# Full-width products near four-column-tile products issued as four 32-column tiles

## The chip, the cores and the metric

The kernel runs on one core of a Trainium2 chip. The metric is the device time of one execution in microseconds (us). Before the change it is 253.65 us (median of three runs, 252.73 to 253.94). Most executions of one kernel agree within about 1%; a run that is over 1.5% above the fastest of its kernel is called slow and is left out of ratios.

## The reference

Two branches of a sequence of 2048 tokens with 640 channels are mixed by a gate:

```python
g = sigmoid((x * gate_w).sum(-1, keepdims=True))
a = _A_ref(...)     # 32 heads of 20 channels, 4 segments of 512 tokens:
                    # softmax(q k^T + mask) v inside a segment, plus a memory of the
                    # earlier segments, then  o @ wo   (the output projection)
b = _B_ref(...)     # irfft2(rfft2(x) * (w_r + 1j * w_i))   (the spectral filter)
return g * a + (1 - g) * b
```

## The kernel before

The program is recorded as operations with priorities, a list scheduler puts them in an order for each engine, and they are then emitted with semaphores. One TensorE operation is a list of matmuls:

```python
def mms(self, items, r, w, prio, name="", extra=0.0):
    cost = sum(max(c * PECOL, 27.0) for _, c in items) + extra
    def f(e):
        h = None
        for th, _ in items:
            o_, l_, r_, st, sp_, kw = th()
            h = e.matmul(o_, l_, r_, start=st, stop=sp_, **kw)
        return h
    return self.Sc.op({"pe": (f, cost, 110.0)}, r=r, w=w, prio=prio, name=name)
```

Every matmul reaches the chip as two instructions, a weight load and a matmul (the trace before has 3248 weight loads and, as a few records are missing, 3226 of the 3248 matmuls). TensorE is used in three tilings: full (128 rows by 128 columns), four row tiles (the scores `qk`, contraction over 20 channels), and four column tiles. In column tiles four matmuls with 32 weight columns each run side by side: in the trace before they start a median 3 ns apart, and a set of four, 320 columns wide, starts 136 ns after the one before it, as a full matmul of 320 columns does. The end of the filter uses them, because each 32-row strip needs another moving operand:

```python
# finish_tile: one 128-row output tile, in two halves of 320 columns
for q in range(4):                                   # "Fb": four column tiles
    # out strip 32q..32q+31  <-  fb[:, 32*(4a+q) : +32]^T  @  G[4a+q][:, half]
    ... {"tile_position": (0, 32 * q), "skip_group_check": True}
for c in range(5):                                   # "oproj", same PSUM bank
    if s < 3:   # one full matmul, 320 wide
        ... oT.ap(c * P, [1, P]), self.wo.ap(c * D + hf * 320, [1, 320])
    else:       # last segment: four column tiles
        ... {"tile_position": (0, 32 * q)}
```

The probability-times-value products (`pv`) are full matmuls that are only 21 wide: 40 of them for a group of four heads.

```python
# pv_group, one item: weights = a 128x128 block of probabilities, moving = 21 columns of values
(self.ps(bank, i*88 + hh*VW, [1, DH+1]), self.ex.ap(... , [1, P]), va.ap(... , [1, DH+1]), ...)
```

The softmax here doesn't subtract the row's maximum and nothing guards it: scores larger than these inputs give would overflow.

## Time and profile before

| | before |
|---|---|
| time, median of 3 | 253.65 us |
| matmuls in the program | 3248 |
| changes of tiling between neighbouring matmuls | 216 |
| last stretch, 197.4 to 249.3 us | TensorE without a break |

PE is TensorE's matmul side and PEld its weight loads. In the page, the chain of waits is followed back from the last instruction; its first line gives shares of the span by engine:

```profile
PE 57%; DVE 19%; DMA 10%; ACT 5%; SPq 3%; issue 3%; POOL 1%; ACTq 0%; DVEq 0%
```

The listing of the same chain in order of time (start, length, what) has its longest piece near the end:

```profile
197.38 51.87 PE psum L593 x867
```

867 matmuls follow each other with nothing else on the chain, so TensorE time saved after 197 us shortens the kernel. The windows view of the kernel before (length, then busy us and instruction count per engine, granted clock, DMA share, GB/s) agrees:

```profile
core 0: us, PE busy (x) PEld busy (x) DVE busy (x) ACT busy (x) POOL busy (x), PEclk, DMA share, GB/s
197.00:240.00 43.00, 42.77 (x642) 24.75 (x640) 24.94 (x66) 34.58 (x30) 18.15 (x28) 1.00 0.35 76
...
230.00:240.00 10.00, 10.00 (x199) 6.50 (x199) 5.43 (x14) 7.57 (x6) 5.85 (x9) 1.00 0.29 84
```

What a change of tiling costs is read from the timeline of TensorE before (start, length, instruction, weights and columns in use, shape, count):

```profile
216.80 0.32 PE L593 MATMUL psum<-G,fbg 128*32 128x320 bf16 x4
217.05 0.85 PE L593 MATMUL psum<-wo,oT 128*128 128x320 bf16 x5
217.84 0.32 PE L593 MATMUL psum<-G,fbg 128*32 128x320 bf16 x4
218.09 0.31 PE L593 MATMUL psum<-wo,oT 128*128 128x320 bf16 x1
```

In this trace a full matmul of 512 columns takes 216 ns from its start to the next one's, and one of 320 columns takes 136 ns (80 ns for 192 columns, which is the 2.4 GHz of the prediction). Four column tiles of 320 columns, where more column tiles follow, take 136 ns too, but the full matmul behind them here starts 0.25 us after them. The missing 0.11 us is the change of tiling. Behind five full matmuls it is the same (0.79 us for 5 x 0.136).

The page's line for an instruction queue (packets, MB, share of 16 engines) is taken for TensorE's: its 25 packets of 16 KB are one for about 260 of the 2 x 3248 weight loads and matmuls:

```profile
q8 instruction: 25, 0.41, 0.7%
```

### The profile page before, as it was taken

The page shows a single profiled execution, that of the slowest core. Times are in us where ns is not written, and L with a number is a line of the kernel's source. Part 1 is how long each engine was busy: PE and PEld are TensorE (multiplying, and loading weights), DVE is VectorE, ACT ScalarE, POOL GpSimd, SP SyncE. Part 2 cuts the span into 40 slices and gives each one's busy share as a digit, 9 for nine tenths or more (in the row PEclk, how much of TensorE's full clock was granted, in tenths as well). Part 3 has the DMA queues.
Part 4 walks back from the last instruction along what each step waited for, and adds up shares of the span by engine and source line. Part 5 has one row for each costly group of instructions (what it writes and reads, how often), then busy time and mean ns, then how long its engine had stood idle before and what let it go on. Part 6 is the DMA issues. An engine that isn't in the chain of part 4 may idle for free.

```text
span 253.9 us, 7958 instructions
## 1 busy us (share of the span) xinstructions
PE 235.9 (93%) x3226; PEld 138.4 (55%) x3248; DVE 202.2 (80%) x556; ACT 203.1 (80%) x208; POOL 114.4 (45%) x175
## 2 busy tenths in 40 slices
PE   7999999989999989989989999999997999999993
PEld 2344556544665547644646566545563656456583
DVE  0789799759998899999999988979999984625543
ACT  2397499958999898999988889889889798788710
POOL 8004735523533336745255747535575532416400
PEclk9999999979999999999999999999999999999998
DMA  7997979599479366656238385313666303464223
GB/s 173 358 355 216 216 173 225 121 205 221 101 112 227 79 168 189 159 125 191 64 96 182 70 204 141 101 44 114 134 169 153 70 3 84 92 115 94 78 68 103
DMA packets 56003, 36.76 MB, mean 145 GB/s; under 512 B 31792, under 2 KB 52256, under 8 KB 55968
## 3 DMA queue, kind: packets, MB, share of 16 engines
q1 hardware_dynamic: 54272, 35.45, 57.6%
q10 hardware_dynamic: 1696, 0.82, 1.2%
q8 instruction: 25, 0.41, 0.7%
q14 instruction: 10, 0.08, 0.2%
HBM read 19.86 MB, written 9.84 MB: 117 GB/s over the span
## 4 chain that ended last, share of the span: by engine, by line
PE 57%; DVE 19%; DMA 10%; ACT 5%; SPq 3%; issue 3%; POOL 1%; ACTq 0%; DVEq 0%
PE psum L593 57%; ACT ex L1183 4%; DMA xsb<-in_A_x_dram 4%; DVE Pt L1333 3%; DMA pkn<-phk 3%; SPq L622 2%; DVE va L1089 2%; DVE xsb L913 1%; SPq L620 1%; DMA tt<-tab_tt 1%; DVE Cp L603 1%; DVE qu L603 1%; DVE xf L908 1%; DMA q_scr<-qu 1%; DMA Wt<-in_B_w_i_dram 1%
## 5 line engine op out<-in xcount | busy, mean ns | idle before, releaser
L1183 ACT ACTIVATE ex<-psum 128x2048 bf16<-128x2048 f32 x80 | 150.3, 1879 | 17.9 <-PE psum L593 17.3
L1186 POOL TENSOR_SCALAR_AFFINE_SELECT ex<-ex 128x512 bf16<-128x512 bf16 x128 | 80.7, 647 | 110.7 <-ACT ex L1183 109.3
L593 PEld LDWEIGHTS psum<-va,ex 128*128 128x128 bf16 x1280 | 36.6, 96 | 7.2 <-POOL ex L1186 2.5
L593 PE MATMUL psum<-va,ex 128*128 128x21 bf16 x1280 | 38.6, 173 | 1.7 <-POOL ex L1186 0.6
L593 PE MATMUL psum<-qp,kp 20*128 20x512 bf16 (+3 forms) x512 | 31.9, 303 | 1.5 <-ACT ex L1183 0.6
L593 PE MATMUL psum<-wv,xT 128*128 128x141 bf16 (+1 forms) x160 | 28.0, 306 | 1.5 <-DVE qu L603 0.6
L1333 DVE TENSOR_TENSOR Pt<-psum,Wt 128x642 bf16<-128x642 f32 x32 | 25.6, 822 | 2.7 <-PE psum L593 1.6
L593 PE MATMUL psum<-xT,wk 128*128 128x512 bf16 (+1 forms) x127 | 25.6, 384 | 2.1 <-DVE qu L603 0.8
L593 PE MATMUL psum<-xT,wq 128*128 128x512 bf16 (+1 forms) x132 | 26.5, 380 | 0.7 <-issue 0.4
L593 PE MATMUL psum<-wo,oT 128*128 128x320 bf16 x120 | 22.1, 301 | 0.0
L593 PEld LDWEIGHTS psum<-qp,kp 20*128 20x128 bf16 x512 | 9.0, 92 | 20.4 <-ACT ex L1183 10.7
L593 PEld LDWEIGHTS psum<-wv,xT 128*128 128x128 bf16 x160 | 13.0, 98 | 10.5 <-issue 1.2
L593 PE MATMUL psum<-big,Cp 128*128 128x321 bf16 (+1 forms) x96 | 17.2, 302 | 1.0 <-DVE eo L603 0.4
L1054 ACT ACTIVATE et<-qu 128x512 bf16<-128x512 bf16 x25 | 15.7, 635 | 2.5 <-DVE qu L603 2.4
L603 DVE CAST ot<-psum 128x320 bf16<-128x320 f32 x19 | 9.1, 490 | 10.6 <-PE psum L593 9.4
L1089 DVE TENSOR_TENSOR va<-psum,ebx 128x500 bf16<-128x500 f32 (+1 forms) x32 | 15.2, 482 | 2.8 <-PE psum L593 1.7
L593 PEld LDWEIGHTS psum<-xT,wk 128*128 128x128 bf16 (+1 forms) x140 | 9.7, 98 | 13.5 <-issue 2.7
L1379 DVE TENSOR_TENSOR G<-eo,psum 128x320 bf16<-128x320 f32 x32 | 14.7, 476 | 2.5 <-PE psum L593 2.4
L593 PEld LDWEIGHTS psum<-xT,wq 128*128 128x128 bf16 (+1 forms) x140 | 10.0, 97 | 11.3 <-issue 1.3
L1218 DVE TENSOR_TENSOR on<-psum,rs 128x320 bf16<-128x320 f32 x32 | 15.5, 483 | 0.3
L593 PE MATMUL psum<-big,Ac 128*128 128x161 bf16 (+2 forms) x96 | 14.5, 257 | 1.3 <-DVE qu L603 0.9
L593 PE MATMUL psum<-tt,Yt 128*128 128x256 bf16 (+1 forms) x96 | 15.0, 273 | 0.3
(80 smaller groups left out, 357.2 us busy)
## 6 DMA issues: line engine op xcount, KB each, us to landing
tt<-tab_tt SPq DMA_DIRECT2D x16, 256.0 KB, 2.9
xsb<-in_A_x_dram SPq DMA_DIRECT2D x8, 320.0 KB, 6.9
qp<-q_scr SPq DMA_DIRECT2D x28, 80.0 KB
kp<-k_scr SPq DMA_DIRECT2D x28, 80.0 KB
o_scr<-on SPq DMA_DIRECT2D x12, 160.0 KB
out_dram<-ot SPq DMA_DIRECT2D x12, 160.0 KB
q_scr<-qu SPq DMA_DIRECT2D x6, 256.0 KB
k_scr<-qu SPq DMA_DIRECT2D x6, 256.0 KB, 2.8
```

Source lines behind the costliest of these rows:

```text
L593: h = e.matmul(o_, l_, r_, start=st, stop=sp_, **kw)
L603: alts["dve"] = (lambda e: e.tensor_copy(dst(), src()), 75 + 1.04 * n, 85.0)
L620: return e.dma_start_transpose(d_, s_)
L622: return e.dma_start(d_, s_)
L908: self.either(lambda e, r=r, op=op: e.tensor_tensor(xf.ap(r * 642, [321, 2], [1, 320]), xs.ap(o, [D, 2], [1, 320]), xs.ap(o + 320, [D, 2], ...
L1054: self.one("act", lambda e: e.activation(et.ap(0, [1, L]), qsl(), ACT.Exp), L, [qb], [b("et", pi_)], late, name="phi_exp")
L1089: self.one("dve", lambda e: e.tensor_tensor(va.ap(i * H * VW + h0 * VW, [VW, nh], [1, DH]), self.ps(bank, 0, [DH, nh], [1, DH]), self.ebx. ...
L1183: self.one("act", lambda e: e.activation(dst(), src(), ACT.Exp, scale=SC), 4 * width, [bank], [self.exb(s, g, j) for g, j in outs], prio - ...
L1186: self.one("pool", lambda e, g=g, j=j: e.affine_select(self.ex.ap(self.exo(s, g) + JOFF[j], [1280, 4], [1, P]), self.ex.ap(self.exo(s, g) ...
L1218: self.one("dve", lambda e, rs=rs, bank=bank, g=g: e.tensor_tensor(on.ap(80 * g, [D, 4], [DH, 4], [1, DH]), self.ps(bank, 0, [88, 4], [VW, ...
L1333: self.one("dve", lambda e, ri=ri, Pt=Pt, Wt=Wt, bank=bank: e.tensor_tensor(Pt.ap(ri * 322, [644, 2], [1, KD]), self.ps(bank, 0, [0, 2], [ ...
L1379: self.one("dve", lambda e, q=q, n2=n2, bank=bank, eo=eo: e.tensor_tensor(self.G.ap(n2 * D + 639 * q, [1 - 2 * q, 320]), eo.ap(q, [1, 320] ...
```

## The change

The intent is to change tiling less often. After scheduling, a greedy pass gives each group of operations that share PSUM banks a mode, full (0) or column tiles (2), with one unit of cost for each change of tiling and 0.03 for each operation in column tiles. A full matmul in mode 2 is issued as four of 32 weight columns. Some modes are fixed: warm-up and gate are full, scores are row tiles, filter product, last projection and a few query and key products are column tiles. The output projection of the first three segments shares its PSUM bank with the filter product and so becomes column tiles with it; the greedy pass chooses for the groups without a fixed member.

```diff
+    def set_modes(self):
...
+        def cost(ops):
+            ids = {o.id for o in ops}
+            c = 0.03 * sum(o.mode == 2 for o in ops)
+            for o in ops:
+                p, n = nbr[o.id]
+                c += (p is not None and p.mode != o.mode) + (n is not None and n.id not in ids and n.mode != o.mode)
+            return c
...          (greedy: runs of 1 to 3 groups are set to 0 or 2 while the cost falls)
     def mms(...):
                 o_, l_, r_, st, sp_, kw = th()
-                h = e.matmul(o_, l_, r_, start=st, stop=sp_, **kw)
+                if mode >= 0 or op.mode != 2:
+                    h = e.matmul(o_, l_, r_, start=st, stop=sp_, **kw)
+                    continue
+                pitch, m = l_.ap[1]
+                for q in range(0, m, 32):
+                    n = min(32, m - q)
+                    dst = bass.AP(tensor=o_.tensor, offset=o_.offset + q * o_.ap[0][0], ap=[[o_.ap[0][0], n]] + [list(d) for d in o_.ap[1:]])
+                    wt = bass.AP(tensor=l_.tensor, offset=l_.offset + q * pitch, ap=[list(l_.ap[0]), [pitch, n]])
+                    h = e.matmul(dst, wt, r_, start=st, stop=sp_, **{**kw, "tile_position": (0, q), "skip_group_check": True})
...
                 self.Sc.schedule({"qk": [0, 1, 2, 3], "gen": [4, 5, 6, 7]}, self.PLAN)
+                self.Sc.set_modes()
```

More of the change, by code (lines that the diff above doesn't have):

```diff
@@ L48 @@
     __slots__ = ("id", "alts", "preds", "succs", "prio", "banks", "nbytes", "npred", "eng", "t0", "t1",
-                 "stamp", "need_inc", "dyn", "first", "outside", "name", "dma", "key", "xfer", "lock")
+                 "stamp", "need_inc", "dyn", "first", "outside", "name", "dma", "key", "xfer", "lock", "mode")
 class Sched:
@@ L68, in op @@
         o.alts, o.prio, o.nbytes, o.name, o.dma = alts, prio, nbytes, name, dma
-        o.xfer, o.lock = xfer, lock
+        o.xfer, o.lock, o.mode = xfer, lock, 0
         o.key = self.keys.setdefault((self.group, name), len(self.keys))
@@ L325, in schedule @@
         self.nsem = nsem
+    def set_modes(self):
+        pe = [o for o in self.order if o.eng == "pe"]
+        banks = {}
+        for o in pe:
+            for b in o.banks:
+                banks.setdefault(id(b), []).append(o)
+        flex = [g for g in banks.values() if all(o.mode < 0 for o in g)]
+        for g in banks.values():
+            for o in g:
+                if o.mode < 0:
+                    o.mode = 2 if any(q.mode == 2 for q in g) else 0
+        nbr = {o.id: (p, n) for p, o, n in zip([None] + pe[:-1], pe, pe[1:] + [None])}
+        def cost(ops):
[5 more added lines that the diff above has]
+            return c
+        moved = True
+        while moved:
+            moved = False
+            for i, g in enumerate(flex):
+                for k in (1, 2, 3):
+                    ops = [o for q in flex[i:i + k] for o in q]
+                    old = [o.mode for o in ops]
+                    c0 = cost(ops)
+                    for m in (0, 2):
+                        for o in ops:
+                            o.mode = m
+                        c1 = cost(ops)
+                        if c1 < c0 - 1e-9:
+                            c0, old, moved = c1, [m] * len(ops), True
+                    for o, m in zip(ops, old):
+                        o.mode = m
     def pe_slow(self, now, occ):
@@ L582, in ps, with mms @@
                        ap=[[4096, np_]] + [list(q) for q in dims])
-    def mms(self, items, r, w, prio, name="", extra=0.0):
+    def mms(self, items, r, w, prio, name="", extra=0.0, mode=-1):
         cost = sum(max(c * PECOL, 27.0) for _, c in items) + extra
@@ L592, in f @@
                 o_, l_, r_, st, sp_, kw = th()
-                h = e.matmul(o_, l_, r_, start=st, stop=sp_, **kw)
-            return h
-        return self.Sc.op({"pe": (f, cost, 110.0)}, r=r, w=w, prio=prio, name=name)
+                if mode >= 0 or op.mode != 2:
[7 more added lines that the diff above has]
+                    h = e.matmul(dst, wt, r_, start=st, stop=sp_, **{**kw, "tile_position": (0, q), "skip_group_check": True})
+            return h
+        op = self.Sc.op({"pe": (f, cost, 110.0)}, r=r, w=w, prio=prio, name=name)
+        op.mode = mode
+        return op
     def copy_alts(self, dst, src, n, engines=("act", "dve"), scale=None):
@@ L816, in warm_up @@
             self.mms([(lambda k=k: (self.ps(bank, 0, [1, L]), t.ap(0, [1, P]), t.ap(P, [1, L]), True, True, {}), 1000)],
-                     [b("warm"), bank], [], -1.0, name="warm")
+                     [b("warm"), bank], [], -1.0, name="warm", mode=0)
     NWARM = 16
@@ L973, in proj_direct @@
                 items.append((th, L / 4))
-            self.mms(items, [b("w" + which + "a"), xb[c], bank], [], prio + (0.0 if c < 3 else 0.45), name="projd")
+            self.mms(items, [b("w" + which + "a"), xb[c], bank], [], prio + (0.0 if c < 3 else 0.45), name="projd", mode=2)
         self.Sc.op(self.copy_alts(lambda: pad.ap(g * L, [1, L]), lambda: self.ps(bank, 0, [1, L]), L),
@@ L1001, in gate @@
             items.append(((lambda n_=n_, part=part: (self.ps(bank, 0, [1, P], np_=4), part(), self.fcat.ap(P, [1, P]), n_ == 0, n_ == 1, {})), P))
-        self.mms(items, [b("hi", s), b("lo", s), b("fcat"), bank], [], prio + 4.0, name="gateT")
+        self.mms(items, [b("hi", s), b("lo", s), b("fcat"), bank], [], prio + 4.0, name="gateT", mode=0)
         self.one("dve", lambda e: e.tensor_copy(self.gT.ap(0, [1, P], np_=4), self.ps(bank, 0, [1, P], np_=4)), P, [bank], [b("gT")],
@@ L1171, in qk_unit @@
                 outs.append((g, j))
-        o = self.mms(items, rb + [bank], [], prio - self.QK_LEAD, name="qk")
+        o = self.mms(items, rb + [bank], [], prio - self.QK_LEAD, name="qk", mode=1)
         fn, occ, lat = o.alts["pe"]
@@ L1427, in finish_tile @@
                 items.append((th, 80))
-            self.mms(items, [b("fbg", s % 3), bank] + last + [b("G", 4 * a + q, hf) for q in range(4)], [], prio, name="Fb", extra=80.0)
+            self.mms(items, [b("fbg", s % 3), bank] + last + [b("G", 4 * a + q, hf) for q in range(4)], [], prio, name="Fb", extra=80.0, mode=2)
             for c in range(5):
@@ L1443, in finish_tile @@
                     ob = [b("oTl", c)]
-                self.mms(items, ob + [b("wo"), bank], [], prio, name="oproj")
+                self.mms(items, ob + [b("wo"), bank], [], prio, name="oproj", mode=2 if s == 3 else -1)
             self.Sc.op(self.copy_alts(lambda hf=hf: ot.ap(hf * 320, [1, 320]), lambda bank=bank: self.ps(bank, 0, [1, 320]), 320),
```

## The prediction

> **What bounds the kernel now.** The chain of waits charges 57% of the 253.9 us span to TensorE. Until 197 us it alternates between engines and DMA. From 197.38 us on it is one uninterrupted TensorE piece: 51.87 us, 867 matmuls, up to the last copies and stores. The windows view agrees: from 197 to 240 us TensorE is busy 42.8 of 43 us, VectorE 24.9, ScalarE 34.6. TensorE time saved there shortens the kernel.

> **What the change does.** The instruction order is unchanged. In the two built programs the tiling changes between neighbouring matmuls 216 times before and 172 times after: 44 switches fewer, all in the last 52 us, around the filter product (already four-tile) and the output projection. In exchange 373 full matmuls become 1492 of 32 columns: 120 output projection (320 wide), 33 inverse column transforms (321), 20 transposes (128) and 200 probability-times-value matmuls (21 wide). The count goes from 3248 to 4367.

> **Gain.** [...] The timeline shows it: from the start of the last matmul before a switch to the first after it, the time beyond columns/2.4 GHz is a median 96 ns into column tiles and 109 ns out of them, against 2 to 6 ns within a mode. So 44 switches cost about 4.5 us (estimate from these gaps). Between two score units the gain can be capped: matmul, 1.88 us exponential and hand-over need about 2.4 us, and the intervals are 2.4 to 2.9 us. I expect 3.5 to 4.5 us to arrive.

> **Cost.**
> - Wide products: a set of four tiles of 320 columns takes 136 ns start to start in the last segment's projection, as does a full 320-wide matmul. Loss under 0.3 us.
> - The 21-wide matmuls are the risk. Today one costs 25 ns with its weight load. As a set, four matmuls and four loads must issue. Tiles of a set start 4 ns apart in the trace, and the load-to-matmul distance of 23 ns could be shared: then a set takes 28 to 35 ns, and 200 sets cost 0.6 to 2 us. If each small matmul costs its 25 ns in sequence, a set takes 100 ns and the cost is 15 us. The trace has no sustained run of small sets; I expect about 40 ns, 3 us.
> - Some 2240 more TensorE instructions: the instruction queue moves 16 KB packets in 1.0 to 1.5 us, about 256 instructions each. A burst of small sets could outrun it, by half a microsecond in all (estimate).

> **Sum.** 253.65 - 4.2 + (most likely 1.5 to 2.5) + 0.3: about **251.3 us**, range **249.3 to 257.5**, skewed upward by the small sets. Chances: faster by over 2% 0.06 (the whole gain is only 1.8%), within 2% 0.79, slower by over 2% 0.15.

> **What would show it.** In the last 52 us the filter-to-projection distance falls from 0.24 to about 0.14 us, and projection sets stay at 136 ns. The 21-wide sets after 200 us run at 28 to 40 ns; at 100 ns the sequential case holds. Before 197 us nothing differs beyond noise. If intervals between score units stop at 2.4 us and ScalarE no longer waits for TensorE, the cap binds. TensorE gaps without a releaser near instruction packets would show fetch stalls.

> **What would make it wrong.** Small sets issuing sequentially; column-tiled weight loads slower than the 93 to 97 ns of the contiguous 32-column loads now, and exposed (strided ones already take 139 ns); instruction fetch stalling; or the tail being bound by the score-exponential loop.

The cost of a change of tiling, medians of 96 and 109 ns, is read from the trace.

## The result, and the profile after

The kernel takes 269.59 us (median of 4 runs, 268.51 to 270.78), against 253.8 us for the kernel before in the same rounds. The ratio is 1.062, with a 95% interval of 1.056 to 1.069: clearly slower. Ratios here are the mean time of one kernel's fast runs over that of the other's of the same rounds, so they are not quite the ratio of the quoted medians.

To place the difference, the same matmul of the program was found in both traces. From the start of a matmul in the first group of probability-times-value products of the tail (at 197.8 us before) to that of the last matmul it takes 51.9 us before and 66.7 us after; up to there the two differ by 1.4 us, in the change's favour and within noise. So 14.8 us are lost in the tail, where the change acts.

First, what the change was for did happen. The timeline of TensorE after:

```profile
218.60 0.31 PE L632 MATMUL psum<-G,fbg 128*32 128x320 bf16 x4
218.74 0.85 PE L639 MATMUL psum<-wo,oT 128*32 128x320 bf16 x20
219.42 0.31 PE L632 MATMUL psum<-G,fbg 128*32 128x320 bf16 x4
219.55 0.31 PE L639 MATMUL psum<-wo,oT 128*32 128x320 bf16 x4
```

From filter product to projection it is now 0.14 us in place of 0.25, and the five projection sets (20 matmuls) take 0.68 us, which is 0.136 us a set. But further on TensorE stands still:

```profile
229.04 0.54 PE L639 MATMUL psum<-va,ex 128*32 128x21 bf16 x48
229.41 0.33 PE L639 MATMUL psum<-wo,oT 128*32 128x320 bf16 x4
229.55 0.34 PE L639 MATMUL psum<-va,ex 128*32 128x21 bf16 x26
230.50 1.03 PE L639 MATMUL psum<-va,ex 128*32 128x21 bf16 x86 [0.61 <-issue]
231.37 0.60 PE L639 MATMUL psum<-wo,oT 128*32 128x320 bf16 x12
231.78 0.40 PE L639 MATMUL psum<-va,ex 128*32 128x21 bf16 x30
234.78 0.29 PE L639 MATMUL psum<-va,ex 128*32 128x21 bf16 x18 [2.60 <-issue]
234.90 0.32 PE L632 MATMUL psum<-G,fbg 128*32 128x320 bf16 x4
235.15 0.40 PE L632 MATMUL psum<-qp,kp 20*128 20x384 bf16 x8
235.48 0.95 PE L639 MATMUL psum<-va,ex 128*32 128x21 bf16 x98
238.23 0.28 PE L639 MATMUL psum<-va,ex 128*32 128x21 bf16 x14 [1.80 <-issue]
```

The brackets are idle time and what ended it. "issue" means that nothing in the profile did: no semaphore, no DMA of data. Two things are worth reading off. The small sets themselves are quick when they run: 86 matmuls, 21.5 sets, from 230.50 to 231.37 us; over the whole trace the median from set to set is 33 ns. And the gaps break into the middle of a set of four: 26, 30 and 98 matmuls are 6.5, 7.5 and 24.5 sets. The waits view sums them for the tail of the kernel after (total us, times, longest):

```profile
PEld psum L639 <- issue: 14.3, 18, 2.7
...
PE psum L639 <- issue: 10.8, 7, 2.6
```

Second, the clock. The windows view after, to be held against the 10.00 busy us at clock 1.00 above:

```profile
230.00:240.00 10.00, 5.10 (x306) 4.12 (x310) 2.41 (x8) 2.91 (x2) 3.72 (x6) 0.78 0.30 87
240.00:250.00 10.00, 7.95 (x339) 5.39 (x330) 3.64 (x9) 4.96 (x5) 1.86 (x3) 0.88 0.09 24
250.00:260.00 10.00, 7.72 (x247) 6.05 (x250) 2.63 (x6) 0.03 (x1) 0.00 (x0) 0.66 0.09 32
```

The clock records behind these means show two stretches of 6.83 us at half clock, 235.6 to 242.4 and 252.7 to 259.5 us. In them a 320-wide set takes 267 ns, against 136 ns at full clock. The kernel before has no half clock in its tail (granted clock 1.00 from 197 to 250 us). The page's line of the instruction queue has grown:

```profile
q8 instruction: 34, 0.56, 0.9%
```

Nine packets more for 2 x (4367 - 3248) = 2238 more instructions: about 249 instructions to a packet of 16 KB.

The trace has the start of each packet. Counting TensorE's recorded weight loads, matmuls and waits in order of their start, the seven long gaps without a releaser lie here (this table is worked out from the trace, it is no view of the profile):

```
TensorE stands still   instructions started so far   modulo 256   last packet's start   gap ends after it
201.51 -> 203.16       5291                          171          200.74                2.42
229.72 -> 230.50       6827                          171          228.00                2.50
232.00 -> 234.78       7083                          171          231.87                2.91
236.25 -> 238.23       7339                          171          235.83                2.40
245.47 -> 246.21       7851                          171          243.84                2.37
248.33 -> 250.12       8107                          171          247.34                2.78
251.32 -> 253.67       8363                          171          251.34                2.33
```

All seven lie at the same place of a grid of 256 instructions, and each ends 2.3 to 2.9 us after a packet started. The next packet starts 1.0 to 1.4 us after a gap's end, and no two packets of the whole run start closer than 3.46 us. (Of this trace's 4367 matmuls 22 are not recorded; with them the place is 193.)

### The profile page after: what moved, and what is told of

The parts are those of the page before. It is cut to its first block, busy times and chain, and to the rows that moved or that the text cites. A ratio compares the mean times of both kernels' runs of the same rounds, so it can differ in the third digit from the quotient of the medians.

```text
span 267.4 us, 10196 instructions
## 1 busy us (share of the span) xinstructions
PE 239.1 (89%) x4345; PEld 145.5 (54%) x4367; DVE 202.5 (76%) x556; ACT 203.1 (76%) x208; POOL 114.7 (43%) x175
## 4 chain that ended last, share of the span: by engine, by line
PE 62%; DVE 14%; DMA 8%; issue 6%; ACT 4%; SPq 2%; POOL 1%; ACTq 0%; DVEq 0%
PE psum L632 51%; PE psum L639 11%; DVE Pt L1382 4%; ACT ex L1232 3%; DMA pkn<-phk 3%; SPq L670 2%; DMA oT<-o_scr 2%; DVE va L1138 2%; DMA Wt<-in_B_w_i_dram 1%; DVE Cp L651 1%; DMA tt<-tab_tt 1%; DMA kp<-k_scr 1%; DVE qu L651 1%; DVE Yt L1387 1%; DVE mem L1175 1%
## 5 line engine op out<-in xcount | busy, mean ns | idle before, releaser
L1232 ACT ACTIVATE ex<-psum 128x2048 bf16<-128x2048 f32 x80 | 150.1, 1877 | 24.9 <-PE psum L632 24.2
L632 PEld LDWEIGHTS psum<-va,ex 128*128 128x128 bf16 x1080 | 30.5, 96 | 6.0 <-POOL ex L1235 2.1
L632 PE MATMUL psum<-va,ex 128*128 128x21 bf16 x1080 | 32.1, 172 | 1.6 <-DVE rs L1265 0.4
L639 PE MATMUL psum<-wo,oT 128*32 128x320 bf16 x480 | 23.5, 313 | 0.8 <-DMA oT<-o_scr 0.8
L649 ACT ACTIVATE ot<-psum 128x320 bf16<-128x320 f32 x13 | 5.5, 435 | 17.4 <-PE psum L632 14.6
L1262 DVE TENSOR_TENSOR rs<-psum,gate 128x16 f32<-128x16 f32 x32 | 5.3, 167 | 17.0 <-PE psum L639 13.4
L639 PE MATMUL psum<-va,ex 128*32 128x21 bf16 x800 | 9.2, 178 | 9.3 <-issue 9.3
L639 PEld LDWEIGHTS psum<-wo,oT 128*32 128x32 bf16 x480 | 12.9, 100 | 5.6 <-issue 1.5
```

The source lines that it names most:

```text
L639: h = e.matmul(dst, wt, r_, start=st, stop=sp_, **{**kw, "tile_position": (0, q), "skip_group_check": True})
L649: alts["act"] = (lambda e: e.activation(dst(), src(), ACT.Copy), 100 + 0.833 * n, 95.0)
L1232: self.one("act", lambda e: e.activation(dst(), src(), ACT.Exp, scale=SC), 4 * width, [bank], [self.exb(s, g, j) for g, j in outs], prio - ...
L1262: self.one("dve", lambda e, rs=rs, bank=bank: e.tensor_tensor(rs.ap(16, [4, 4], [1, 4]), self.ps(bank, DH, [88, 4], [VW, 4]), self.g1.ap(4 ...
```

## The experiments

All kernels gave correct results.

### Small products left full: e1_small_full

```diff
-                         prio, name="pv")
+                         prio, name="pv", mode=0)
```

> The change, but the 21-wide probability-times-value products stay full matmuls (3728 matmuls, 184 tiling switches instead of 4367 and 172). Theory F (instruction fetch: TensorE gets its instructions in 16 KB blocks of 256, the next block takes about 3.5 us to come, so a block that is worked off faster leaves TensorE waiting at the block's end): no block of this kernel is shorter than 3.5 us, so no long gap without a releaser, no half clock in the last 52 us, and 32 switches at 0.10 us are saved: about 250.4 us (estimate), faster than before by 1.2%. Rival S (the 21-wide four-tile sets themselves are what stalls): the same. Rival C (column tiles as such are slow here, the wide ones too): most of the 16 us stays, 260 us or more.

Measured: 253.39 us median (6 runs; 252.5 us for the four fast ones), ratio to before 0.994 (0.988 to 1.001). There is no gap without a releaser in the tail (the longest such wait is 0.3 us, of a weight load) and no half clock (0.999 granted over the profiled run). So rival C is out: 252 column-tiled sets in place of 92 do no harm. F and S both allow this result. But the tail is only 1.5 us shorter than before (50.4 against 51.9), not 3.2; this is taken up below.

### Small products alone in column tiles: e2_small_only

```diff
+        for o in pe:                 # after the greedy pass
+            if o.name != "pv":
+                o.mode = 0
```

> Only the five 21-wide head groups as four-tile sets, all other products as before (3848 matmuls, 225 switches). Theory F: around the small sets stand full matmuls with few instructions, so the blocks are longer; walking the built order with 3.5 us a block gives 4.7 us of gaps, plus 0.9 us for 9 more switches and 1.6 us for sets of 33 ns: about 261 us, gaps again at one fixed place modulo 256 instructions. Rival S: the gaps belong to the small sets, so the same 12 us of gaps and the half clock as in the change: 270 us or more, and gaps at no fixed place in the instruction count.

Measured: 265.92 us median (5 runs), ratio 1.045 (1.038 to 1.052). The profiled run is slow (270.74 us), so its trace is read for positions, and for sizes only roughly: four gaps without a releaser, 6.6 us from start to start (F had forecast 4.7), all at 193 modulo 256. The five groups have the same small sets as in the change, yet fewer and shorter gaps, at block ends. That is F's picture, but the time, 265.0 to 267.6 us in fast runs, lies between the two forecasts: F's 261 us had left the half clock out, and fast runs show a mean clock of 0.973 to 0.987 here against 0.991 to 0.999 for those of before. By time alone this run would not have decided.

### No small sets, but twice the instructions: e4_proj_halves

On top of the first experiment, each projection set is cut into two of 160 columns.

```diff
+                for c in (0, 160) if name == "oproj" else ():
+                    for q in range(0, m, 32):
+                        dst, wt, mv = (strip q, columns c..c+159), (weights of strip q), (moving columns c..c+159)
+                        h = e.matmul(dst, wt, mv, start=st, stop=sp_, ...)
```

> The first experiment (small products full), with each four-tile set of the output projection of the first three segments cut into two sets of 160 columns: the same arithmetic time, twice the instructions (4208 matmuls), and no 21-wide four-tile set. Theory F: 256 instructions of such sets last 2.2 us, under 3.5, so gaps appear at block ends: 5.1 us by walking the order, 5 to 7 us slower than the first experiment, about 256 us. Rival S: no small set, no gap; within 1 us of the first experiment.

Measured: 259.78 us median (4 runs), ratio 1.023 (1.017 to 1.029). Fast runs against fast runs, that is 7.3 us above the first experiment (252.5 us). In the traces the tail is 4.7 us longer; the rest lies before the tail, where nothing was changed: this run was at half clock there for 6.8 us, the profiled run of the first experiment not at all. The timeline of its TensorE has gaps inside the projection:

```profile
220.35 0.37 PE L647 MATMUL psum<-wo,oT 128*32 128x160 bf16 x9
221.20 0.73 PE L647 MATMUL psum<-wo,oT 128*32 128x160 bf16 x31 [0.48 <-issue]
...
223.44 0.85 PE L647 MATMUL psum<-wo,oT 128*32 128x160 bf16 x37
225.48 0.25 PE L647 MATMUL psum<-wo,oT 128*32 128x160 bf16 x3 [1.18 <-issue]
```

There are seven such gaps, 6.0 us from start to start, all at 193 modulo 256 (no matmul record is missing in this trace, so this is the same place as in the change). Not one 21-wide column tile is in the program. Rival S does not survive: the arithmetic was unchanged, only the number of instructions went up. The clock stayed full in this tail (the 6.8 us at half clock before it account for the run's mean granted clock of 0.987), so the loss here is the gaps alone.

### The same work on a shifted grid: e5_shifted

```diff
-  (warm-up: 16 full matmuls of 512 columns)
+  (warm-up: 12 of them, and 4 x 16 of 16 columns: 120 instructions more, before any data is there)
```

> The change with 120 more TensorE instructions at the very start: four of the sixteen warm-up matmuls are replaced by sixteen 16-column ones each, while TensorE waits for data anyway. Nothing after that is touched. Theory F: the long gaps still end at one fixed place modulo 256 of the instruction count (171, as in the change; any other place for a fixed count would also do, but one place), that is, at other matmuls of the program than before, 120 instructions earlier in the work; the sum of gaps stays 10 to 13 us (12.2 by walking the order), time 266 to 272 us. Rival S, and any rival that ties a gap to certain matmuls or to a semaphore: the gaps stay at the same matmuls.

Measured: 270.58 us median (4 runs), ratio 1.059 (1.051 to 1.067), 1.063 to fast runs alone. Six gaps without a releaser in the tail, 12.1 us from start to start, all at 172 in the recorded count. This trace lacks 21 matmul records where that of the change lacks 22, so both are 193. They hit other work. One falls into the row-tiled scores, which were never changed:

```profile
241.73 0.39 PE L636 MATMUL psum<-qp,kp 20*128 20x256 bf16 x6
243.73 0.28 PE L636 MATMUL psum<-qp,kp 20*128 20x256 bf16 x2 [1.61 <-issue]
```

A gap that is tied to certain matmuls or to a semaphore would have stayed where it was. It is tied to the instruction count.

### Pauses in place of starved blocks: e6_pauses

On top of the first experiment, waits on a count that ScalarE had long reached are put at seven places of TensorE's order, where the change has its gaps.

```diff
+            if e == "pe":
+                for at, us in self.GAPS:      # seven places
+                    if self.npe < at <= self.npe + o.nmm:
+                        for _ in range(round(us / 0.055)):
+                            self.eng[e].wait_ge(prog["act"], 1)
```

> The first experiment (no small four-tile sets, no starved block) with seven pauses of TensorE, about 11 us in all (10 to 14 us; 138 waits on a semaphore count long reached), at the seven places where the change has its gaps. If idle TensorE time is what lowers the clock (theory K): the trace shows half clock for some 7 to 14 us in the last 60 us although no tile is small and no block short, and the time is 253 + 11 + 3 to 6 = 266 to 270 us. If the half clock comes from the small tiles: the clock stays full and the time is about 264 us.

Measured: 268.04 us median (4 runs), ratio 1.050 (1.042 to 1.059), 1.055 to fast runs alone; 15.9 us above the fast runs of the first experiment (252.2 us). The waits view charges 8.9 us of TensorE's idle time to the pauses (six times "issue"), and all of its idle time in the tail is 11.0 us. The clock fell just as in the change, for 13.65 us in the tail, in stretches of 10.24 and 3.41 us:

```profile
220.00:230.00 10.00, 8.58 (x236) 5.57 (x232) 2.03 (x5) 8.15 (x7) 4.15 (x6) 1.00 0.83 107
230.00:240.00 10.00, 6.17 (x124) 3.44 (x120) 3.41 (x10) 1.88 (x1) 2.21 (x4) 0.53 0.19 63
240.00:250.00 10.00, 7.19 (x180) 5.00 (x180) 3.41 (x8) 4.96 (x5) 1.86 (x3) 0.95 0.13 38
250.00:260.00 10.00, 8.62 (x220) 7.20 (x224) 4.24 (x10) 0.77 (x2) 0.00 (x0) 0.83 0.14 42
```

The first experiment run again has full clock in the same stretch:

```profile
230.00:240.00 10.00, 9.28 (x272) 6.66 (x269) 5.72 (x15) 6.62 (x6) 4.12 (x7) 1.00 0.25 84
```

So idle time put into TensorE's order is enough to halve the clock, without small tiles, and it costs more than the idle time itself: the tail is 13.8 us longer than in the first experiment run again, with 9.4 us more of idle time. The other 4.4 us fit the clock (half of the 13.65 us less the 4.0 us of idle time in them is 4.8 us, an estimate). K holds in this sense, with two limits. First, two more stops, 0.45 us up to 215.69 and 0.79 us up to 226.16, lie on the grid of 256 (at 171 in the recorded count). Their packets began 2.2 and 3.3 us after the block before was entered, in place of about 1.1 us, so this run is not wholly free of fetch waits, and the 3.5 us of a fetch are not a constant. Second, which idle time trips the clock is not shown: the first half-clock stretch begins at 230.68 us, just as the longest pause begins, and e4 kept full clock in its tail with seven gaps of up to 1.2 us.

### The projection alone: e3_proj_only

```diff
+        for o in pe:                 # after the greedy pass
+            if o.name != "oproj":
+                o.mode = 0
```

> Only the output projection as four-tile sets; the inverse transforms, the transposes and the 21-wide products stay full (3608 matmuls, 198 switches). Theory F: no gaps, 18 switches saved at 0.10 us: 251.9 us, 0.7% faster than before, and 1.4 us slower than the first experiment. If the switch cost is not what is saved [...], it equals before.

Measured: 253.75 us median (6 runs), ratio 0.998 (0.992 to 1.004). In its trace the tail is 50.4 us, 1.5 us shorter than before: the 18 switches (1.8 us by estimate) arrive there almost whole. In the whole time this is lost in run-to-run noise. The forecast difference from the first experiment did not show in the tail: both are 50.4 us.

### The first experiment again, and with more output buffers: e1_again, e7_more_ot

```diff
-        self.ot = [TL(f"ot{i}", [P, D]) for i in range(4)]
+        self.ot = [TL(f"ot{i}", [P, D]) for i in range(6)]
+  (after scheduling, so that the order stays: a copy into a buffer waits for the store
+   six tiles back in place of four)
```

> The first experiment once more, to be compared with the six-buffer kernel in the same rounds: 0.4 to 1.0% faster than before.

> The first experiment with six output buffers in place of four, same instruction order. In its trace a store that took 7.8 us held an output buffer, so ScalarE copied and exponentiated late and TensorE waited 1.2 us near 237 us. [...] 1 to 1.5 us faster than the first experiment, and no TensorE wait of a microsecond in the last 52 us. If the store was only late in that one run: no difference beyond 0.5 us.

Measured: 252.53 us for the first experiment (6 runs, one of them slow; ratio 0.990, 0.983 to 0.996) and 253.02 us with six buffers (6 runs, ratio 0.991, 0.984 to 0.997). To the fast runs of the kernel before alone the ratios are 0.994 (about 0.988 to 0.999, worked out from the listed runs) and 0.996. The first experiment is thus about 0.6% faster than the kernel before, barely clear of noise, and the best kernel. Six buffers bring nothing: the tail is 50.6 us without and 50.4 us with them. In the trace with six buffers VectorE waits 4.95 us for a store and TensorE 0.9 us for VectorE, elsewhere. The forecast of 1 to 1.5 us was wrong; the wait moved.

Where did the rest of the saved switches go? Waits of the weight loads in the tail, before:

```profile
PEld psum L593 <- issue: 6.9, 29, 0.3
PEld psum L593 <- ACT ex L1183: 1.2, 4, 0.4
...
PEld psum L593 <- POOL ex L1186: 0.4, 2, 0.2
```

and in the first experiment run again:

```profile
PEld psum L632 <- ACT ex L1232: 3.2, 11, 0.4
...
PEld psum L632 <- POOL ex L1235: 1.3, 2, 1.1
PEld psum L639 <- DMA oT<-o_scr: 0.8, 1, 0.8
```

Waits with no releaser fall from 6.9 to 3.9 us (2.3 for line 632 and 1.6 for line 639), while waits for the exponentials grow by 2.0 us, for the mask by 0.9, and for a load of the projection's input from nothing to 0.8. That a faster TensorE reaches these sooner is a reading of the two traces; no run took those waits away, so it is not shown which of them binds.

## Why the prediction was wrong

| step of the prediction | forecast | runs |
|---|---|---|
| tail bound by TensorE | yes | right: all of the loss is there |
| 44 switches fewer at 0.10 us | 4.5 us | distance right (0.25 to 0.14 us); about half of it arrives where nothing starves (e1: 32 switches, 3.2 us by estimate, tail 1.3 to 1.5 us shorter) |
| wide sets keep 136 ns | under 0.3 us lost | right: median 136 ns |
| small sets | 28 to 35 ns if shared, 40 budgeted | right: 33 ns, 1.6 us for 200 |
| instruction fetch | half a microsecond in all | **wrong: 10.8 us idle** |
| clock | not mentioned | half clock for 13.65 us, about 5 us lost (estimate) |

The step that failed is the one on fetching: "A burst of small sets could outrun it, by half a microsecond in all (estimate)." The cause was named and its term in the sum was mis-sized by a factor of twenty. The packet's own length, 1.0 to 1.5 us in the prediction (0.93 to 1.57 us in the trace before, median 1.18), was apparently taken for the time that a fetch needs. By theory F what counts is the whole round, about 3.5 us, of which the packet is a part: in the change's trace no two packets start closer than 3.46 us, and the next one starts only 1.0 to 1.4 us after a gap's end, so each block has to last that long by itself. Walking the recorded blocks with at least 3.5 us for each gives 12.2 us of gaps for the change (12.1 us measured, from start to start) and 0 for the kernel before. The 3.5 us themselves come from the change's trace: in the kernel before no two packets start closer than 4.8 us, so it could be foreseen that blocks would become short (256 instructions in sets of 28 to 35 ns last about 1 us), but not read from that trace how long a fetch takes.

The small sets got the attention and were not slow. At 33 ns a set, 256 of their instructions last 1.06 us (worked out from the median), against 3.46 us from packet to packet: by theory F they starve their own instruction stream.

The second part is the clock. At half clock the tail spends 13.65 us; about 2.8 us of that TensorE stands still and 0.8 us (99 small matmuls, 25 sets of 33 ns) run no slower than at full clock (a median 33 ns a set in the first of the two stretches, 32 ns from 197 us up to it), so about half of the remaining 10 us, 5 us, is lost (an estimate from these records).

The balance of the tail, then, in estimates from the traces: -4.5 us for switches, +1.6 for small sets, +10.8 for starved blocks, +5.0 for the clock, +0.8 for a wait on a load (220.9 to 222.1 us): 13.7 of the measured 14.8 us. The remaining 1 us stays open. Two terms are loose: from start to start the gaps are 12.1 us rather than 10.8 (the ends of matmuls are modelled), and of the switches only about half may arrive, as in the first experiment.

## What to carry to other kernels

Splitting a matmul into four tiles saved a change of tiling here (0.25 to 0.14 us from filter product to projection) but multiplies instructions (4367 matmuls in place of 3248), and instructions have a supply rate of their own: in the change no two packets of about 256 TensorE instructions started closer than 3.46 us. Before splitting, count instructions per microsecond over each stretch of 256, and give a cost function the number of instructions, not of operations: the change charged an operation of 16 small matmuls no more than one of a single wide matmul. Gaps without any releaser at a fixed place modulo 256 of the instruction count are put down to fetches here: in the change they ended 2.3 to 2.9 us after a packet's start, and in e5 they moved to other work with the count. And where single stops of about 2 us or more were among them (the change and e5, and the pauses of e6) part of the tail also ran at half clock (13.65 us of it in the change and in e6; e5's granted clock over the whole run is 0.981), while seven gaps of up to 1.2 us (e4) left the clock alone.
